# A PSUM bank for the weight conversion and a new interleaving of layers 3 and 4, in a fused attention and MLP kernel

## The chip, the cores and the metric

The kernel runs on one core of a Trainium2 chip, as one launch. The metric is the device time of the launch in microseconds (us). Three runs before gave 752.56 us as median (752.18 to 753.29).

The engines are named as in the profile: PE is TensorE (matmuls; PEld its weight loads), DVE is VectorE, ACT is ScalarE, POOL is GpSimd, SP is SyncE, which here only issues DMAs. SBUF is the large on-chip memory, PSUM the small one of eight banks of 128 x 512 fp32 into which PE writes. Each engine works through its own instructions strictly in the order of the program and waits where an input, or a buffer, isn't ready.

## What is computed

Batch 2, 8 heads, 768 positions, head size 64: an attention in which a query sees only the keys of its own hash bucket, and then two MLPs on 1536 tokens of width 512. The weights come as float64.

```python
attn = softmax(where(bucket(q) == bucket(k), q @ k.T / 8, -1e9)) @ v   # 16 heads
x = attn, heads side by side                                           # 1536 x 512
h = maximum(maximum(x @ w1, x @ w2), x @ w3)                           # 1536 x 768   "layer 1"
x = h @ w_out                                                          # 1536 x 512   "layer 2"
u = x @ w_in                                                           # 1536 x 2048  "layer 3"
g = where(u >= 1, u, where(u <= -1, 0, (u + 1) ** 2 / 4))
out = g @ w_out2                                                       # 1536 x 512   "layer 4"
```

## The kernel before

**Precision.** Every fp32 factor is split into a high part (a cast to the fast matmul type fp32r) and a low part (the rest), and each product is three matmuls: high x high, high x low, low x high (`PARTS`, `mm3`). A high part is made by ACT, the low part by POOL, which subtracts.

**Weights.** There are 58 slices of a weight matrix, 128 x 512 or 128 x 384, in the order in which they are needed: 18 of layer 1, 8 of layer 2, then by turns two of layer 3 and two of layer 4. `w_steps(n)` turns one from float64 into fp32 parts. It is a generator that stops (`yield`) after each instruction or two, and `w_tick(k)`, called at many places of the program, runs k of these pieces, so conversion is strewn into the other work. A slice takes: a DMA of the raw slice (L196, two raw buffers), ACT's square of the upper words into the tile `wg` (L208), four DVE instructions (L210, L215, L219, L223), ACT's cast to the high part (L231), POOL's subtraction to the low part (L262). `wg` has two buffers in SBUF, the result `wg2` too; finished slices lie in seven buffers (`w`, `wx`), and `w_done` says which are free again. `w_get` converts at once what isn't ready when a product wants it.

**Block products.** The last 14 slices of layer 1 and all of layer 3 are done in pairs of slices by a scheme with seven products instead of eight. `pair_units` has eleven units of six matmuls; I number them u0 to u10. They need sums and differences of the two weight slices (`sr`, DVE, L242 to L247; split by ACT L254 and POOL L256 into two tiles `s`) and of the tokens (`x_d`). Between the units partial results move: u0's bank is copied by ACT into a second one (L1046); u3's goes to `x7` (L1057); DVE adds `x7` to the bank of u4 and so makes the start of u9 (L1062), before u7 may write that bank again; after u7 ACT copies its bank, for u10 (L1072). A tile `s` is not written before `w_state["open"]` allows it, and until then no further slice is begun (L249).

**Layers 3 and 4.** Nine steps (L1248). Step i does pair i of layer 3 (`l3`) and, for pair i-1, the twelve token tiles of layer 4 (`l4`, six matmuls each; I call them T0 to T11), which are added up in SBUF in `acc`. A string of 3s and 4s (L1253) sets the order of units and tiles. g is made of each layer 3 result by ACT (L1191, L1192), DVE (L1193), ACT (L1202) and POOL (L1203). Of a step's twelve tiles DVE adds eight to `acc` (L1238). The other four (`SEEDED`) go another way: ACT copies the old sum into the bank (L1222), the matmuls add to it there, and ACT copies the bank back (L1236).

**Banks.** After the attention PE's outputs rotate through eight PSUM banks, `b0` to `b5`, `u_ps` and `pj_ps`; `bank()` takes the one that has been free longest.

**Start.** After the attention layer 1's first four slices are multiplied plainly (`l1`, L1117), three chunks of tokens each, while `steps` (L1098) makes the token differences: two of them per chunk.

## Time and profile before

| | |
|---|---|
| median of three runs | 752.56 us |
| the profiled execution, its own time | 752.83 us |
| its span, first to last instruction | 750.8 us |
| PE busy | 671.3 us (89%) |
| DVE, ACT, POOL busy | 536.2, 428.9, 367.9 us (71, 57, 49%) |
| mean granted TensorE clock | 0.952 of full |
| attention, to the first unit of layer 1 | about 0 to 205 us |
| layer 1, plain part and seven pairs | 205 to 380 us |
| layer 2 | 380 to 429 us |
| layers 3 and 4 | 429 to 751 us |

PE's share is high everywhere, so what counts is where it waits, and where it runs at a lower granted clock; both are read by stretches. The views that answer this are the table of stretches (busy time and granted clock), PE's waits with what ended them, and the timeline. What an instruction costs is read from the groups by line and shape.

### The profile page before, as it was taken

How to read it: one execution, taken by the hardware profiler on the slowest of the kernel's cores; microseconds unless marked ns; L12 is line 12 of the kernel's file. 1: busy time of each engine (PE TensorE's matmuls, PEld its weight loads, DVE VectorE, ACT ScalarE, POOL GpSimd, SP SyncE). 2: the span in 40 equal slices, each digit the busy share in tenths (PEclk: the TensorE clock that was granted, in tenths of full speed). 3: DMA queues.
4: the chain of work that ended last, by engine and by line, in shares of the span. 5: the costliest groups of instructions: out<-in, count | busy, mean ns of one | idle time of the engine just before them, and what ended most of it. 6: DMA issues, size and time to landing. Idle time of an engine off the chain costs nothing.

```text
span 750.8 us, 11606 instructions
## 1 busy us (share of the span) xinstructions
PE 671.3 (89%) x4323; PEld 524.3 (70%) x4323; DVE 536.2 (71%) x775; ACT 428.9 (57%) x796; POOL 367.9 (49%) x313
## 2 busy tenths in 40 slices
PE   7999999999999489889899983989798989898998
PEld 5667777778787367667688862867576767676776
DVE  5788899998549688897755874675767676666633
ACT  7787778877622435444433563665556565646562
POOL 6435575653324764664343465353635363626340
PEclk9999999999999799999999996989899999899999
DMA  7856776862321112112202011111120202021004
GB/s 194 207 145 183 199 203 191 240 158 82 86 71 57 56 57 84 57 56 64 82 24 85 28 57 56 57 56 57 33 81 28 85 28 85 28 67 46 29 0 169
DMA packets 27856, 66.99 MB, mean 89 GB/s; under 512 B 4164, under 2 KB 9124, under 8 KB 27800
## 3 DMA queue, kind: packets, MB, share of 16 engines
q1 hardware_dynamic: 27488, 66.21, 29.7%
q8 instruction: 34, 0.56, 0.3%
q14 instruction: 22, 0.18, 0.1%
q10 hardware_dynamic: 312, 0.04, 0.0%
HBM read 46.17 MB, written 3.19 MB: 66 GB/s over the span
## 4 chain that ended last, share of the span: by engine, by line
PE 50%; DVE 22%; ACT 16%; POOL 6%; issue 5%; DMA 0%; DVEq 0%; ACTq 0%; POOLq 0%
PE b L299 13%; PE s_ps L440 5%; PE b L1230 5%; PE t_ps L473 5%; DVE wg L223 5%; PE u_ps L534 5%; DVE wg L210 5%; PE s_ps L443 4%; DVE wg L219 4%; DVE wg L215 4%; ACT r L1191 3%; PE u_ps L1230 3%; ACT wg L208 2%; PE u_ps L501 2%; ACT r L1192 2%
## 5 line engine op out<-in xcount | busy, mean ns | idle before, releaser
L1203 POOL TENSOR_TENSOR g<-r,g 128x512 fp32r<-128x512 f32 x48 | 66.1, 1378 | 92.7 <-ACT g L1202 75.1
L210 DVE SCALAR_TENSOR_TENSOR wg<-wg,wr 128x512 f32<-128x512 f32 (+1 forms) x58 | 68.0, 1173 | 53.7 <-ACT wg L208 53.6
L450 DVE TENSOR_SCALAR_CACHE_REDUCE p<-s_ps 128x768 f32<-128x768 f32 x96 | 89.8, 951 | 13.3 <-PE s_ps L443 9.9
L465 ACT ACTIVATE p<-p,nm 128x768 f32<-128x768 f32 x96 | 89.7, 936 | 6.8 <-DVE p L450 6.3
L440 PE MATMUL s_ps<-lo,q 128*128 128x384 f32 x192 | 72.5, 378 | 2.9 <-POOL lo L407 2.0
L299 PE MATMUL b<-x_d,s 128*128 128x512 f32 x204 | 56.1, 415 | 21.3 <-DVE b L1062 7.5
L299 PE MATMUL b<-x_hl,wx 128*128 128x512 f32 x288 | 74.2, 402 | 0.6 <-POOL wx L262 0.6
L1230 PE MATMUL b<-w,g 128*128 128x512 f32 (+1 forms) x207 | 56.3, 407 | 17.6 <-ACT w L231 10.1
L299 PE MATMUL b<-x_hl,w 128*128 128x512 f32 (+1 forms) x324 | 71.3, 371 | 0.0
L299 PEld LDWEIGHTS b<-x_hl,wx 128*128 128x128 f32 x288 | 56.8, 198 | 13.6 <-POOL wx L262 1.0
L262 POOL TENSOR_TENSOR wx<-wg,wx 128x512 fp32r<-128x512 f32 (+1 forms) x32 | 44.8, 1399 | 43.6 <-ACT wx L231 41.6
L443 PE MATMUL s_ps<-hi,q 76*128 76x384 f32 x192 | 66.1, 344 | 0.0
L299 PEld LDWEIGHTS b<-x_hl,w 128*128 128x128 f32 x324 | 56.7, 191 | 10.9 <-issue 0.6
L299 PEld LDWEIGHTS b<-x_d,s 128*128 128x128 f32 x204 | 39.7, 199 | 33.3 <-DVE b L1062 9.2
L1230 PE MATMUL b<-wx,g 128*128 128x512 f32 x159 | 48.0, 436 | 15.7 <-ACT b L1222 13.2
L219 DVE SCALAR_TENSOR_TENSOR wg<-wg,wg 128x512 int32<-128x512 int32 (+1 forms) x58 | 59.3, 1023 | 1.2
L1230 PEld LDWEIGHTS b<-w,g 128*128 128x128 f32 x207 | 39.8, 196 | 27.8 <-ACT w L231 10.5
L1193 DVE SCALAR_TENSOR_TENSOR r<-r,b 128x512 f32<-128x512 f32 x36 | 24.6, 684 | 47.4 <-ACT r L1192 47.4
L231 ACT CAST wx<-wg 128x512 fp32r<-128x512 f32 (+1 forms) x32 | 19.3, 603 | 66.2 <-DVE wg L223 66.2
L256 POOL TENSOR_TENSOR s<-sr,s 128x512 fp32r<-128x512 f32 x30 | 42.6, 1432 | 24.8 <-ACT s L254 24.8
L223 DVE SCALAR_TENSOR_TENSOR wg<-wr,wg 128x512 int32<-128x512 int32 (+1 forms) x58 | 53.1, 916 | 1.2
L215 DVE TENSOR_SCALAR wg<-wg 128x512 int32<-128x512 int32 (+1 forms) x58 | 49.2, 847 | 3.5
(184 smaller groups left out, 1596.7 us busy)
## 6 DMA issues: line engine op xcount, KB each, us to landing
wr<-in_w SPq DMA_DIRECT2D x48, 512.0 KB
r<-in_kq SPq DMA_DIRECT2D x15, 384.0 KB
q<-hi SPq DMA_DIRECT2D x15, 384.0 KB
v<-in_v SPq DMA_DIRECT2D x21, 256.0 KB
rb<-d SPq DMA_DIRECT2D x16, 192.0 KB
wr<-in_w SPq DMA_DIRECT2D x8, 384.0 KB
q<-lo SPq DMA_DIRECT2D x15, 192.0 KB
lo<-hi SPq DMA_DIRECT2D x15, 192.0 KB
```

The source lines that it names most:

```text
L210: nc.vector.scalar_tensor_tensor(out=f32(g), in0=f32(g), scalar=TINY_SQ, in1=f32(high), op0=ALU.is_ge, op1=ALU.mult)
L215: nc.vector.tensor_scalar(out=g2, in0=g, scalar1=3, scalar2=0x3FFFFFF8, op0=ALU.logical_shift_left, op1=ALU.bitwise_and)
L219: nc.vector.scalar_tensor_tensor(out=g2, in0=g, scalar=-0x40000000, in1=g2, op0=ALU.bitwise_and, op1=ALU.bitwise_or)
L223: nc.vector.scalar_tensor_tensor(out=g2, in0=low, scalar=29, in1=g2, op0=ALU.logical_shift_right, op1=ALU.bitwise_or)
L262: nc.gpsimd.tensor_tensor(out=w[:, 1, 0:cols], in0=f32(g2), in1=f32(w[:, 0, 0:cols]), op=ALU.subtract)
L299: nc.tensor.matmul(out=outp, lhsT=w_[a], rhs=x_[b_], start=(begins and i == 0 and jj == 0), stop=(ends and i == n - 1 and jj == 2), skip_g ...
L440: nc.tensor.matmul(out=o, lhsT=hd["qa"][:, qs], rhs=hd["lo"][:, ks], start=True, stop=False)
L443: nc.tensor.matmul(out=o, lhsT=hd["qb"][0:76, qs], rhs=hd["hi"][0:76, ks], start=False, stop=True)
L450: nc.vector.tensor_scalar(out=p.rearrange("p (a k) -> p a k", a=2), in0=s_ps[bank.at][:, :, 0:HALF], scalar1=MASKED, scalar2=MASKED, op0=A ...
L465: nc.scalar.activation(out=p, in_=p, func=ACTF.Exp, scale=-1.0, bias=tl[n]["nm"], accum_out=sums_of(h // 2)[:, c:c + 1],)
L1203: nc.gpsimd.tensor_tensor(out=lo, in0=r, in1=f32(hi), op=ALU.subtract)
L1230: nc.tensor.matmul(out=pb[:, cs], lhsT=gs[f][:, a, tsl], rhs=wt[:, b_, cs], start=(n == 0 and k not in seeds), stop=(n == len(terms) - 1), ...
```

## The change

Four things are changed.

1. The bank `pj_ps` leaves the rotation, which then has seven banks, and takes the place of `wg`: the square and the first results of DVE lie in it. L219's result now goes there as well, and the last DVE instruction reads it from there. In the attention, where `pj_ps` is in use, `wg` stays in SBUF, with one buffer.
2. The split of a pair's sums is taken out of `w_steps` into a queue of its own (`sums_todo`), of which each `w_tick` runs a piece when `open` allows it. Slices go on being converted meanwhile, up to the next one that would fill `sr`.
3. There are no seeded tiles: layer 4's tiles are added by DVE, all twelve of a step (in the first, i = 0, ACT copies them, as before).
4. The string changes: units stand two by two between single tiles, and eight tiles come after the last unit, where it was one by one and four. Each unit of layer 3 is followed by two ticks, where it was two or one. In layer 1's start there are three token steps per chunk in place of two, and two ticks in place of three for the first four.

```diff
-        g = w_p.tile([128, 512], I32, tag="wg", name="wg", bufs=2)[:, 0:cols]
+        g = w_state["bank"]
+        if g is None:
+            g = w_p.tile([128, 512], I32, tag="wg", name="wg", bufs=1)
+        g = g[:, 0:cols]
...
-            out=g2, in0=g, scalar=-0x40000000, in1=g2, op0=ALU.bitwise_and, op1=ALU.bitwise_or
+            out=g, in0=g, scalar=-0x40000000, in1=g2, op0=ALU.bitwise_and, op1=ALU.bitwise_or
...
-            out=g2, in0=low, scalar=29, in1=g2, op0=ALU.logical_shift_right, op1=ALU.bitwise_or
+            out=g2, in0=low, scalar=29, in1=g, op0=ALU.logical_shift_right, op1=ALU.bitwise_or
...
-        yield
-        while pair_at[n] >= w_state["open"]:
-            yield
-        s_ = [w_state["sums"].tile([128, 2, 2, 256], F32R, tag="s", name="s") for _ in range(2)]
-        sums_w[pair_at[n]] = s_
+        sums_todo.append((pair_at[n], sums_parts(pair_at[n], sr)))
+
+    def sums_parts(m, sr):
+        s_ = sums_w[m] = [w_state["sums"].tile([128, 2, 2, 256], F32R, tag="s", name="s") for _ in range(2)]
         for i in range(2):
...
+    def sums_tick():
+        if sums_todo and sums_todo[0][0] < w_state["open"] and next(sums_todo[0][1], 0) == 0:
+            sums_todo.pop(0)
...
     def w_tick(count=1):
         for _ in range(count):
+            sums_tick()
...
+                if n in pair_at and sums_todo:
                     return
...
-            for n, tile_ in ((6, u_ps), (7, pj_ps)):
-                at_bank[n] = tile_
-                banks.append(n)
+            at_bank[6] = u_ps
+            banks.append(6)
+            w_state["bank"] = i32(pj_ps)
...
-                    l1(j, w, c, slice(S - TCH, TCH) if (j, w, c) in early else slice(0, TCH))
-                    for _ in range(2):
+                    l1(j, w, c, slice(S - TCH, TCH) if (j, w, c) in early else slice(0, TCH), 2 if n < 4 else 3)
+                    for _ in range(3):
...
-                SEEDED = (1, 4, 7, 10)
...
-                        if k + 1 in SEEDED and i > 0:
-                            seeds[k + 1] = bank(True)
-                            nc.scalar.copy(out=seeds[k + 1][1], in_=acc[:, TOKS[k + 1]])
...
-                            if i == 0 or k in seeds:
+                            if i == 0:
                                 nc.scalar.copy(out=acc[:, t, cs], in_=pb[:, cs])
...
-                    for n, x in enumerate("33433434343434343434444"):
+                    for n, x in enumerate("33343343343343343444444" + "4"):
                         next(g3 if x == "3" else g4, None)
                         if x == "3":
-                            w_tick(2 - n % 2)
+                            w_tick(2)
```

The order of instructions up to layer 1 stays as it was. Lines after the change are some ten further down: L208 to L223 are L211 to L226 there, L1062 is L1072, L1238 is L1242.

DVE, at layer 1's start, where the fourth slice is converted (its raw words are `wr_2630`) and the token differences `raw` begin; before:

```order
L210 SCALAR_TENSOR_TENSOR wg_2926<-wg_2926,wr_2630 128x512
L215 TENSOR_SCALAR wg2_2929<-wg_2926 128x512
L219 SCALAR_TENSOR_TENSOR wg2_2929<-wg_2926,wg2_2929 128x512
L223 SCALAR_TENSOR_TENSOR wg2_2929<-wr_2630,wg2_2929 128x512
L1094 TENSOR_TENSOR raw_2904<-x_hl_72 128x1024
L1094 TENSOR_TENSOR raw_2905<-x_hl_72 128x1024
L960 TENSOR_TENSOR h1_2811<-b1_2813,h1_2811 128x256
```

and after:

```order
L213 SCALAR_TENSOR_TENSOR pj_ps_84<-pj_ps_84,wr_2630 128x512
L1104 TENSOR_TENSOR raw_2904<-x_hl_72 128x1024
L218 TENSOR_SCALAR wg2_2945<-pj_ps_84 128x512
L222 SCALAR_TENSOR_TENSOR pj_ps_84<-pj_ps_84,wg2_2945 128x512
L1104 TENSOR_TENSOR raw_2905<-x_hl_72 128x1024
L1027 TENSOR_TENSOR raw_2906<-raw_2904,raw_2906 128x1024
L1027 TENSOR_TENSOR raw_2904<-raw_2905,raw_2904 128x1024
L969 TENSOR_TENSOR h1_2811<-b1_2813,h1_2811 128x256
L226 SCALAR_TENSOR_TENSOR wg2_2945<-wr_2630,pj_ps_84 128x512
```

The slice's last DVE instruction has moved behind five others, four of them token differences of 1024 columns.

PE, at the end of step 4 of layers 3 and 4, before from u8 on and after the change from u9 on (`x_hl` and `x_d` are tokens, `s` sums, `w` and `wx` slices); before:

```order
L299 MATMUL pj_ps<-x_hl,wx 128x512 x6
L1230 MATMUL b_2863<-w,g 128x512 x6
L299 MATMUL b_2813<-x_hl,wx 128x512 x6
L1230 MATMUL b_2849<-w,g 128x512 x6
L299 MATMUL b_2833<-x_hl,s 128x512 x6
L1230 MATMUL u_ps<-w,g 128x512 x6
L1230 MATMUL b_2908<-w,g 128x512 x6
L1230 MATMUL b_2798<-w,g 128x512 x6
L1230 MATMUL pj_ps<-w,g 128x512 x6
```

and after:

```order
L308 MATMUL b_2833<-x_hl,wx 128x512 x6
L308 MATMUL b_2813<-x_hl,s 128x512 x6
L1235 MATMUL b_2849<-w,g 128x512 x6
L1235 MATMUL b_2798<-w,g 128x512 x6
L1235 MATMUL b_2863<-w,g 128x512 x6
L1235 MATMUL u_ps<-w,g 128x512 x6
L1235 MATMUL b_2908<-w,g 128x512 x6
L1235 MATMUL b_2833<-w,g 128x512 x6
L1235 MATMUL b_2813<-w,g 128x512 x6
L1235 MATMUL b_2849<-w,g 128x512 x6
```

The last unit (the one with `x_hl,s`) has moved ahead of four more tiles, and the tiles use the bank `pj_ps` no more.

DVE, in the same part of a step (acc is layer 4's sum); before:

```order
L210 SCALAR_TENSOR_TENSOR wg_5480<-wg_5480,wr_5402 128x512
L1238 TENSOR_TENSOR acc_4322<-u_ps_83,acc_4322 128x512
L215 TENSOR_SCALAR wg2_5491<-wg_5480 128x512
L1238 TENSOR_TENSOR acc_4322<-b5_2908,acc_4322 128x512
L219 SCALAR_TENSOR_TENSOR wg2_5491<-wg_5480,wg2_5491 128x512
L223 SCALAR_TENSOR_TENSOR wg2_5491<-wr_5402,wg2_5491 128x512
L1238 TENSOR_TENSOR acc_4322<-pj_ps_84,acc_4322 128x512
```

and after:

```order
L213 SCALAR_TENSOR_TENSOR pj_ps_84<-pj_ps_84,wr_5290 128x512
L1242 TENSOR_TENSOR acc_4300<-b3_2849,acc_4300 128x512
L218 TENSOR_SCALAR wg2_5407<-pj_ps_84 128x512
L222 SCALAR_TENSOR_TENSOR pj_ps_84<-pj_ps_84,wg2_5407 128x512
L226 SCALAR_TENSOR_TENSOR wg2_5407<-wr_5290,pj_ps_84 128x512
L1242 TENSOR_TENSOR acc_4300<-b0_2798,acc_4300 128x512
L1242 TENSOR_TENSOR acc_4300<-b4_2863,acc_4300 128x512
L1242 TENSOR_TENSOR acc_4300<-u_ps_83,acc_4300 128x512
```

Three additions now follow each other where two stood apart, and each conversion instruction has one operand in `pj_ps`.

## Rows read from the trace of the kernel before

**Rows 1.** The page, part 4: the chain that ended last, by engine.

```profile
PE 50%; DVE 22%; ACT 16%; POOL 6%; issue 5%; DMA 0%; DVEq 0%; ACTq 0%; POOLq 0%
```

**Rows 2.** Stretches: start:end, length, busy us (instructions) by engine, PEclk, DMA, GB/s.

```profile
230.90:271.15 40.25, 26.87 (x99) 20.47 (x97) 30.29 (x40) 15.87 (x26) 22.44 (x14) 0.83 0.18 61
271.15:378.30 107.15, 95.45 (x397) 76.03 (x396) 89.28 (x109) 46.69 (x87) 60.30 (x44) 0.97 0.20 66
378.30:428.62 50.32, 50.32 (x223) 41.70 (x222) 33.33 (x41) 19.49 (x36) 21.76 (x16) 1.00 0.16 50
428.62:446.84 18.22, 15.84 (x67) 12.16 (x66) 14.03 (x18) 11.16 (x20) 10.46 (x8) 1.00 0.18 59
446.84:496.25 49.41, 36.23 (x140) 28.11 (x138) 28.16 (x34) 30.18 (x54) 26.53 (x21) 0.83 0.13 43
496.25:543.58 47.33, 37.66 (x140) 28.85 (x138) 30.90 (x40) 26.67 (x47) 20.98 (x16) 0.86 0.16 56
543.58:696.91 153.33, 135.27 (x554) 108.13 (x552) 103.69 (x140) 91.10 (x160) 71.76 (x52) 0.94 0.16 55
696.91:750.80 53.89, 48.56 (x217) 39.46 (x215) 22.53 (x33) 24.57 (x44) 14.54 (x11) 1.00 0.18 69
```

**Rows 3.** PE's waits from 543.58 to 696.91: us in total, times, longest.

```profile
PE b L1230 <- ACT b L1222: 13.9, 4, 3.5
PE u_ps L1230 <- ACT u_ps L1222: 4.1, 4, 1.0
```

**Rows 4.** The timeline, PE: start, length, what [idle before <- what ended it].

```profile
459.86 0.80 PE L1230 MATMUL b<-w,g 128*128 128x512 f32 x1 [10.11 <-ACT w L231]
...
577.21 4.61 PE L1230 MATMUL b<-wx,g 128*128 128x512 f32 x12 [3.49 <-ACT b L1222]
...
705.11 1.52 PE L299 MATMUL b<-x_d,s 128*128 128x512 f32 x6
706.47 1.52 PE L1230 MATMUL pj_ps<-wx,g 128*128 128x512 f32 x6
```

**Rows 5.** PE's waits in layer 1 from 230.9 to 378.3.

```profile
PE b L299 <- DVE b L1062: 7.5, 4, 2.5
PE b L299 <- POOL s L256: 5.9, 1, 5.9
PE b L299 <- ACT s L254: 4.4, 1, 4.4
PE b L299 <- ACT b L1072: 3.6, 3, 2.4
PE b L299 <- DVE pj_ps L1062: 2.0, 1, 2.0
```

**Rows 6.** DVE's groups from 205 us on, by shape: out<-in xcount | busy us, mean ns.

```profile
L210 DVE SCALAR_TENSOR_TENSOR wg<-wg,wr 128x512 f32<-128x512 f32 x47 | 55.5, 1182 | 41.8 <-ACT wg L208 41.6
L219 DVE SCALAR_TENSOR_TENSOR wg<-wg,wg 128x512 int32<-128x512 int32 x47 | 51.3, 1091 | 1.0
L223 DVE SCALAR_TENSOR_TENSOR wg<-wr,wg 128x512 int32<-128x512 int32 x47 | 46.3, 986 | 1.0
L215 DVE TENSOR_SCALAR wg<-wg 128x512 int32<-128x512 int32 x47 | 39.5, 841 | 2.6
L1193 DVE SCALAR_TENSOR_TENSOR r<-r,b 128x512 f32<-128x512 f32 x36 | 24.6, 684 | 47.4 <-ACT r L1192 47.4
L1238 DVE TENSOR_TENSOR acc<-b,acc 128x512 f32<-128x512 f32 x29 | 19.9, 685 | 18.3 <-PE b L1230 18.3
...
L1062 DVE TENSOR_TENSOR b<-b,x 128x512 f32<-128x512 f32 x11 | 7.6, 690 | 0.8 <-ACT x L1057 0.6 <-PE b L299 0.2
...
L1018 DVE TENSOR_TENSOR raw<-raw 128x1024 f32<-128x1024 f32 x4 | 4.9, 1220 | 0.0
```

**Rows 7.** The timeline of one step, DVE and POOL.

```profile
589.30 1.29 POOL L1203 TENSOR_TENSOR g<-r,g 128x512 fp32r<-128x512 f32 x1 [5.94 <-ACT g L1202]
589.35 1.78 DVE L223 SCALAR_TENSOR_TENSOR wg<-wr,wg 128x512 int32<-128x512 int32 x1
...
595.94 0.68 DVE L223 SCALAR_TENSOR_TENSOR wg<-wr,wg 128x512 int32<-128x512 int32 x1
...
598.56 0.41 DVE L244 TENSOR_TENSOR sr<-wg,sr 128x256 f32<-128x256 f32 x1
598.89 0.41 DVE L246 TENSOR_TENSOR sr<-wg 128x256 f32<-128x256 f32 x1
```

**Rows 8.** The timeline at layer 1's start.

```profile
222.36 5.39 POOL L1094 TENSOR_TENSOR raw<-x_hl 128x1024 f32<-128x1024 f32 x2
...
222.98 2.51 DVE L215 TENSOR_SCALAR wg<-wg 128x512 int32<-128x512 int32 x1
...
231.04 2.90 PE L299 MATMUL u_ps<-x_hl,wx 128*128 128x512 f32 x12
```

**Rows 9.** The page, part 5: ACT's cast and POOL's subtraction.

```profile
L262 POOL TENSOR_TENSOR wx<-wg,wx 128x512 fp32r<-128x512 f32 (+1 forms) x32 | 44.8, 1399 | 43.6 <-ACT wx L231 41.6
...
L231 ACT CAST wx<-wg 128x512 fp32r<-128x512 f32 (+1 forms) x32 | 19.3, 603 | 66.2 <-DVE wg L223 66.2
```

More of the change, by code (lines that the diff above doesn't have):

```diff
@@ L178, in lsh_attention_moe_kernel @@
     pair_at = {key_index[b_]: m for m, (_, b_) in enumerate(PAIRS)}
-    g2s, sums_w = {}, {}
-    w_state = {"open": 0, "raw": 0, "done": 0, "base": 0, "gen": None, "auto": False, "more": None}
+    g2s, sums_w, sums_todo = {}, {}, []
+    w_state = {"open": 0, "bank": None, "raw": 0, "done": 0, "base": 0, "gen": None, "auto": False, "more": None}
     def w_piece(n, i):
@@ L271, in w_tick @@
                 if n >= NSL or n >= w_state["base"] + (WBUFS if w_state["more"] else WEARLY):
+                    return
+                if n in pair_at and sums_todo:
                     return
@@ L964, in l1_out, with l1 @@
                     pending.append(lambda: split_h(j, c))
-            def l1(j, w, c, cs=slice(0, TCH)):
+            def l1(j, w, c, cs=slice(0, TCH), ticks=3):
                 wt = w_get(("1", j, w))
@@ L973, in l1 @@
                 free(b, cs.stop - cs.start == TCH)
-                w_tick(3)
+                w_tick(ticks)
             def split_h(j, c):
@@ L1030, in pair_units @@
                 wts = [w_get(k) for k in keys]
-                assert m in sums_w
+                while m not in sums_w or sums_todo and sums_todo[0][0] == m:
+                    sums_tick()
                 s_ = sums_w.pop(m)
@@ L1216, in l4 @@
                     wts = [w_get(("4", f)) for f in fs]
-                    seeds = {}
                     for k, t in enumerate(TOKS):
                         tsl = slice(t * 128, (t + 1) * 128)
-                        if k + 1 in SEEDED and i > 0:
-                            seeds[k + 1] = bank(True)
-                            nc.scalar.copy(out=seeds[k + 1][1], in_=acc[:, TOKS[k + 1]])
                         cuts_ = 2 if i == 7 and k == NT // 128 - 1 else 1
                         for h in range(cuts_):
-                            b = seeds[k] if k in seeds else bank()
+                            b = bank()
                             pb = b[1]
@@ L1231, in l4 @@
                                     out=pb[:, cs], lhsT=gs[f][:, a, tsl], rhs=wt[:, b_, cs],
-                                    start=(n == 0 and k not in seeds), stop=(n == len(terms) - 1),
-                                    skip_group_check=k in seeds,
+                                    start=(n == 0), stop=(n == len(terms) - 1),
                                 )
-                            if i == 0 or k in seeds:
+                            if i == 0:
                                 nc.scalar.copy(out=acc[:, t, cs], in_=pb[:, cs])
```

## The prediction

> **What bounds the kernel now.** The chain that ended last gives PE half of the span, and DVE with ACT 38% [rows 1]: stretches in which PE works alternate with stretches in which it waits for the other two. So I priced PE's work and looked in which stretch more time than that goes by. A unit or a tile is six matmuls; one begins at 705.11 and the next at 706.47, in a stretch with the granted clock at 1.00, so six cost 1.36 us [rows 4]. [...]
>
> Against that stand, by the table of stretches [rows 2]: steps 3 to 6, 153.3 us for 4 x 31.28 = 125.1, so 28.2 over (A). Step 2, 47.3 for 31.3, 16.0 over (B). Step 1, 49.4, 18.1 over (C). Step 0, 18.2 for 11 units or 15.0, 3.3 over (D). Six pairs of layer 1, 107.1 for 66 units or 89.8, 17.4 over (E). The end of layer 1's plain part with its first pair (three chunks of twelve matmuls and ten units, 8.2 + 13.6 = 21.8), 40.2, 18.5 over (F). Layer 2 loses nothing: 50.3 us, all of it busy. The end from 696.9 on waits 2 to 3 us (G), as an estimate from the seed waits of the steps ahead of it.
>
> What is waited for: in A, PE is idle for 153.3 - 135.3 = 18.0 us, and two rows hold it all, 13.9 + 4.1 us in eight waits for L1222, ACT's copies of seeds [rows 3]. The other 10.1 us of A are matmuls at a lower granted clock, 0.94 in the mean. [...] A microsecond waited thus costs another 10.1 / 18.0 = 0.56. In C one wait of 10.11 us is for the first slice of layer 4 [rows 4]. In E and F PE waits for the sums (5.9 and 4.4 us) and for the partial results that DVE and ACT move (7.5, 2.0 and 3.6) [rows 5].
>
> **The change, edit by edit.** *No seeds.* The 28 tiles lose two ACT copies each, and DVE gets 28 additions. The waits of rows 3 go whole, with the clock that they cost. What is late next? The loads of a step answer. ACT has 91.1 / 4 = 22.8 us, less 8 copies at its mean of 91.1 / 160 = 0.57, so 18.2; POOL 71.8 / 4 = 17.9 [rows 2]. DVE will have 16 conversion instructions at 0.69 (next paragraph), 12 additions at 0.685, 6 L1193 at 0.684, one L1062 at 0.69 and four sums at 0.41 [rows 6, 7]: 11.0 + 8.2 + 4.1 + 0.7 + 1.6 = 25.7. All lie under 31.3, so PE becomes the bound, if what it waits for is queued early enough.
>
> *Conversion in a bank.* A slice's four DVE instructions now take 1.18 + 0.84 + 1.09 + 0.99 = 4.10 us in the mean [rows 6]. They are long because two operands in SBUF make DVE wait while POOL runs: L223 took 1.78 us beside POOL's L1203 and 0.68 when POOL was idle [rows 7]. Instructions with one operand in PSUM stand at 0.684 to 0.690 throughout (L1193, L1238, L1062), POOL or not [rows 6]. With the bank each of the four has an operand there. Two of them, L213 and L222, read and write one bank in place, which no row shows. The bounds are L1062, which reads one bank and writes another, 0.69, and the 1.22 us of a 1024-column instruction, as if the two passes followed each other [rows 6]. I take 0.69, since L1062 is the nearest. A slice then takes 2.76, 1.34 less. One buffer in place of two for `wg` loses nothing: one slice is converted at a time, and its square came after the last slice's L223 already.
>
> [...]
>
> *The string.* Units no longer stand one by one with tiles, so each result of layer 3 is split by DVE, ACT and POOL earlier, and eight tiles with 8 x 0.685 us of additions cover 8 x 1.36 us of PE behind them. In a walk along DVE's queue as it is written, DVE comes back to the same place of the next step after 30.8 us if independent instructions start 0.08 us before their forerunner ends (598.89 against 598.56 + 0.41 [rows 7]), and after 33.8 if each waits for the last one's end. So A's loss is 0 to 2.5 us a step; I take 1.0, nearer to the overlap that the row shows, and 4 for A (from 28.2). B has the same, and a tail of C's delay: 1.5 (0 to 4).
>
> For C: the first tile is now behind three units, not two, so it is wanted 1.36 us later, and two slices come 1.34 earlier each. The wait falls from 10.1 to about 6.0, with clock lost 7 in all. If all four slices' gain counts it is 10.1 - 1.4 - 5.4 = 3; with none, 8.7 and a little over 2 of clock, 11. D: 1 (0 to 3).
>
> *Sums queued.* Slices go on while `s` is taken, and the sums' parts no longer stand in a slice's way. In E DVE has 89.3 of 107.1 us [rows 2]; 15 slices at 1.34 less leave 69 of 90. Its queue then has slack, and L1062 waits less. L1072 and other copies of ACT remain. I take 0.8 us a pair, 5 in all. Bounds: 0, and 12, the pairs' waits for DVE and ACT as they are (17.4 less the 5 that slack in a queue gives back at least).
>
> *Start.* Three token steps per chunk push DVE's L226 of the fourth slice behind three differences. L215 began at 222.98 while POOL was on 222.36 to 227.75, and took 2.51 us [rows 8]. In that place now come L1104 1.22, L218 0.69, L222 0.69, L1104 1.22, two L1027 2.44, a 256-column addition, at half of 0.69 about 0.34, and L226 0.69: 7.3 us, so 230.3, and up to 4.8 more if the first one has to wait for POOL. Cast and subtraction add 0.60 + 1.40 [rows 9]: 232.3 to 237.0, and PE wants the slice at 231.04 [rows 8]. That is a new stall of 1 to 6 us; I take 4. The waits for sums, 5.9 + 4.4 [rows 5], mostly go, since they are made while chunks run: 1 left. With 5 for matmuls at the lower clock behind both (the granted clock there is 0.83 [rows 2]) F is 10 (5 to 16). G: 0.5 (0 to 2).
>
> **Sum.** From 28.2 to 4, 16.0 to 1.5, 18.1 to 7, 3.3 to 1, 17.4 to 5, 18.5 to 10, 2.3 to 0.5: 103.8 becomes 29, a gain of 75. The profiled execution's own time of 752.8 (its span is 750.8) agrees with the median of 752.6, so both give 678. All lows together (8) give 657, all highs (10 + 4 + 11 + 3 + 12 + 16 + 2 = 58) 707.
>
> **Rivals.** *Seven banks.* `pj_ps` leaves the rotation, so a bank is wanted again 7 x 1.36 = 9.5 us after it was taken, not 10.9. Eight tiles in a row all need DVE, whose queue has a slice (2.76) or a pair's sums between the additions; where it lags, the next step's u0 waits for the bank of a tile. For it: a step has 25.7 us of DVE in a strict order, and the slower walk was late there. Against: after a slice's four instructions come three additions in a row, 2.1 us for 4.1 of PE. If it holds, the slower walk's 2.5 us a step come over what I took, in six steps 16: 694. [...]
>
> *DVE as slow as before.* The conversion may still wait for POOL, or the in-place ones cost 1.22. Then a slice stays near 4.1, DVE's step is 25.7 + 4 x 1.34 = 31.1, with 41.8 / 47 = 0.9 us of idleness ahead of each L210 [rows 6] 34.7. That is 3.4 over PE's, 5.3 with the clock at 0.56, so 4.3 more than taken in six steps and 6 in the pairs: 710. Against it stand the even 0.68 to 0.69 of all rows with a bank.
>
> *It doesn't do what it says.* Seed waits may only be the visible end of another lag, and steps stay at 38.3: A keeps 28.2 and B much of its loss, so 678 + 24 + 14 = 716. Against: rows 3 hold A's whole idle time, and what is left for ACT and DVE is under PE's work.
>
> *Slower.* It decides in L213 and L222, eight a step: from 0.69 + (38.3 - 25.7) / 8 = 2.3 us each DVE alone fills the 38.3 us that a step takes now, and layer 1's 30 of them make 69 + 30 x 1.6 = 117 us for 107. From there on the kernel is slower than before; at 2.4 us, 39.4 a step and 120 in layer 1 give about 770. Against: no DVE row of 512 columns with a bank in [rows 6] is over 0.69.
>
> **How the numbers follow.** Forecast, 678: 0.70, its own range 657 to 707. Seven banks, 694: 0.12. DVE as slow as before, 710: 0.10. Not what it says, 716: 0.04. Slower, 770: 0.04. The range 657 to 712 holds most of the first and the next two. About 0.2% is what a measurement of this kernel can tell; faster than that holds for all but the slower case and its border: 0.95, within it 0.01, slower 0.04.
>
> **What would show it.** In the changed kernel's profile: L213, L218, L222 and L226 at 0.68 to 0.71 us in the mean; a step's first matmuls 31.3 to 34 us apart; no wait on an ACT copy in the steps, and a granted clock of 0.97 or more; T0 of step 1 waiting 4 to 6 us for a slice; a wait of 1 to 6 us near 231 at the fourth slice's first chunk; pairs 15 to 16 us apart. I am wrong if PE waits for DVE's additions or a bank in each step (seven banks), if the four stay at 0.8 to 1.2 (DVE as slow), or if the in-place ones stand above 1.2.

## The result, and the profile after

The changed kernel takes 672.85 us (median of four runs, 671.09 to 674.23) against 752.92 us: a ratio of 0.8933, with an interval of 0.8905 to 0.8961. The profiled execution has 671.09 us of its own, and a span of 669.3 us where it was 750.8. The prediction was 678, between 657 and 712.

The chain that ended last is now mostly PE's own work, where [rows 1] gave it half:

```profile
PE 79%; DVE 12%; ACT 4%; issue 3%; DMA 1%; POOL 1%; DVEq 0%; ACTq 0%; SPq 0%; POOLq 0%
```

The table of stretches, cut at the same places of the program as [rows 2] (columns as there):

```profile
230.03:260.66 30.63, 25.98 (x97) 19.64 (x96) 27.78 (x37) 15.48 (x26) 20.08 (x12) 0.89 0.26 86
260.66:355.28 94.62, 90.49 (x397) 74.28 (x397) 70.21 (x111) 48.15 (x90) 57.52 (x45) 1.00 0.23 74
355.28:405.60 50.32, 50.32 (x224) 41.67 (x222) 30.32 (x43) 19.53 (x37) 20.13 (x16) 1.00 0.18 57
405.60:423.52 17.92, 15.83 (x67) 12.23 (x66) 13.20 (x20) 12.01 (x23) 12.62 (x10) 1.00 0.12 42
423.52:461.91 38.39, 33.85 (x139) 27.17 (x138) 22.73 (x36) 30.46 (x57) 25.74 (x21) 0.91 0.24 76
461.91:493.19 31.28, 31.28 (x139) 25.90 (x138) 22.89 (x37) 20.45 (x37) 16.82 (x13) 1.00 0.23 76
493.19:618.31 125.12, 125.12 (x553) 103.60 (x552) 97.71 (x157) 73.33 (x128) 67.31 (x52) 1.00 0.21 68
618.31:669.30 50.99, 47.83 (x217) 39.67 (x215) 27.46 (x43) 15.21 (x26) 12.98 (x10) 1.00 0.17 63
```

Steps 2 to 6 take 31.28 us each, and PE is busy for all of it at a granted clock of 1.00: exactly 23 times 1.36 (11 units and 12 tiles). Against [rows 2] the stretches give back, in order, 9.6, 12.5, 0, 0.3, 11.0, 16.0, 28.2 and 2.9 us; with 0.9 ahead of the first that is the 81.5 by which the span is shorter. ([rows 2] begins its first stretch 0.3 us before the end of the chunk at which this table begins; cut alike, that stretch gives 9.3.) The loads of a step came out near those forecast: in steps 3 to 6 ACT is busy for 18.3 us a step (forecast 18.2), POOL for 16.8 (17.9) and DVE for 24.4 (25.7).

What PE still waits for from 200 us on (total, times, longest):

```profile
PE b L1235 <- ACT wx L234: 3.3, 1, 3.3
PE b L308 <- DVE u_ps L1072: 2.6, 2, 2.2
PE b L308 <- DVE b L1072: 1.9, 1, 1.9
PE u_ps L308 <- ACT wx L234: 1.9, 1, 1.9
PE b L1235 <- POOL wx L268: 1.3, 1, 1.3
PE b L308 <- ACT x_hl L1163: 1.2, 1, 1.2
...
PE u_ps L308 <- POOL wx L268: 0.9, 1, 0.9
```

No wait is for a layer 4 addition, or for a bank of the rotation that isn't free yet. Those for L1072, and the two left out for L1056 and L1082 (1.2 and 0.2 us), are for links between the units of a pair. DVE's groups from 200 us on answer [rows 6]: the four conversion instructions, 0.68 to 0.70 us each where they stood at 0.84 to 1.18:

```profile
L222 DVE SCALAR_TENSOR_TENSOR pj_ps<-pj_ps,wg 128x512 int32<-128x512 int32 x47 | 32.8, 697 | 1.2
L213 DVE SCALAR_TENSOR_TENSOR pj_ps<-pj_ps,wr 128x512 f32<-128x512 f32 x47 | 32.7, 697 | 30.0 <-ACT pj_ps L211 30.0
L218 DVE TENSOR_SCALAR wg<-pj_ps 128x512 int32<-128x512 int32 x47 | 32.3, 687 | 2.3
L226 DVE SCALAR_TENSOR_TENSOR wg<-wr,pj_ps 128x512 int32<-128x512 int32 x47 | 32.2, 684 | 1.1
```

### The profile page after: what moved, and what is told of

It reads as the page before. It is cut to its first block, busy times and chain, and to the rows that moved or that the text cites. A ratio compares the mean times of both kernels' runs of the same rounds, so it can differ in the third digit from the quotient of the medians.

```text
span 669.3 us, 11587 instructions
## 1 busy us (share of the span) xinstructions
PE 645.2 (96%) x4323; PEld 513.4 (77%) x4323; DVE 495.6 (74%) x803; ACT 396.6 (59%) x740; POOL 352.8 (53%) x313
## 4 chain that ended last, share of the span: by engine, by line
PE 79%; DVE 12%; ACT 4%; issue 3%; DMA 1%; POOL 1%; DVEq 0%; ACTq 0%; SPq 0%; POOLq 0%
PE b L308 24%; PE b L1235 18%; PE u_ps L308 7%; PE s_ps L449 6%; PE t_ps L482 5%; PE u_ps L543 5%; PE s_ps L452 5%; PE u_ps L510 3%; DVE raw L1027 2%; PE u_ps L1235 2%; PE pj_ps L425 2%; DVE pj_ps L213 1%; DVE wg L226 1%; DVE wg L218 1%; DVE pj_ps L222 1%
## 5 line engine op out<-in xcount | busy, mean ns | idle before, releaser
L459 DVE TENSOR_SCALAR_CACHE_REDUCE p<-s_ps 128x768 f32<-128x768 f32 x96 | 89.7, 951 | 13.3 <-PE s_ps L452 10.0
L1213 POOL TENSOR_TENSOR g<-r,g 128x512 fp32r<-128x512 f32 x48 | 62.7, 1306 | 37.9 <-ACT g L1212 37.7
L308 PE MATMUL b<-x_d,s 128*128 128x512 f32 x270 | 68.6, 398 | 6.4 <-DVE u_ps L1072 2.6
L1235 PE MATMUL b<-wx,g 128*128 128x512 f32 x264 | 67.5, 393 | 4.5 <-ACT wx L234 3.3
L308 PEld LDWEIGHTS b<-x_d,s 128*128 128x128 f32 x270 | 51.2, 192 | 19.6 <-DVE u_ps L1072 3.4
L213 DVE SCALAR_TENSOR_TENSOR pj_ps<-pj_ps,wr 128x512 f32<-128x512 f32 (+1 forms) x55 | 37.2, 677 | 37.5 <-ACT pj_ps L211 37.5
L234 ACT CAST wx<-wg 128x512 fp32r<-128x512 f32 (+1 forms) x32 | 19.4, 605 | 73.3 <-DVE wg L226 73.3
L1235 PEld LDWEIGHTS b<-wx,g 128*128 128x128 f32 x264 | 49.8, 189 | 15.7 <-ACT wx L234 3.7
L268 POOL TENSOR_TENSOR wx<-wg,wx 128x512 fp32r<-128x512 f32 (+1 forms) x32 | 40.7, 1273 | 39.3 <-ACT wx L234 36.1
L308 PE MATMUL b<-x_hl,w 128*128 128x512 f32 (+1 forms) x282 | 59.5, 363 | 0.0
L1242 DVE TENSOR_TENSOR acc<-b,acc 128x512 f32<-128x512 f32 (+1 forms) x77 | 51.6, 677 | 8.9 <-PE b L1235 8.9
L449 PEld LDWEIGHTS s_ps<-lo,q 128*128 128x128 f32 x192 | 36.7, 191 | 21.3 <-DVE p L459 8.6
L492 ACT COPY pt<-t_ps 128x768 f32<-128x768 f32 (+1 forms) x59 | 41.0, 706 | 17.0 <-PE t_ps L482 14.7
L268 POOL TENSOR_TENSOR w<-wg,w 128x512 fp32r<-128x512 f32 (+1 forms) x26 | 33.0, 1269 | 29.9 <-ACT w L234 26.8
```

The source lines that it names most:

```text
L213: nc.vector.scalar_tensor_tensor(out=f32(g), in0=f32(g), scalar=TINY_SQ, in1=f32(high), op0=ALU.is_ge, op1=ALU.mult)
L268: nc.gpsimd.tensor_tensor(out=w[:, 1, 0:cols], in0=f32(g2), in1=f32(w[:, 0, 0:cols]), op=ALU.subtract)
L308: nc.tensor.matmul(out=outp, lhsT=w_[a], rhs=x_[b_], start=(begins and i == 0 and jj == 0), stop=(ends and i == n - 1 and jj == 2), skip_g ...
L449: nc.tensor.matmul(out=o, lhsT=hd["qa"][:, qs], rhs=hd["lo"][:, ks], start=True, stop=False)
L459: nc.vector.tensor_scalar(out=p.rearrange("p (a k) -> p a k", a=2), in0=s_ps[bank.at][:, :, 0:HALF], scalar1=MASKED, scalar2=MASKED, op0=A ...
L492: copy(out=grp[g][:, 3 * a:3 * b_, r * 128:(r + 1) * 128].rearrange("p (a j) q -> p a j q", a=b_ - a), in_=t_ps[:, a:b_, 0:HALF].rearrange ...
```

## The experiments

Every kernel was cut at the same matmuls, so a difference can be put down to a stretch. This table holds the length of each in the profiled execution (worked out from the starts of the matmuls in the timelines; F from the end of the chunk before it, the letters as in the prediction), and the median of the timed runs. F begins 230.0 to 233.8 us into the span, from profile to profile, which says nothing here. Where kernels run the same instructions in a stretch, its length agrees within 0.1 us (F and E of the changed kernel, a_seeds and i_step0).

| kernel | F | E | D | C | B | A | G | median us |
|---|---|---|---|---|---|---|---|---|
| before | 39.9 | 107.2 | 18.2 | 49.4 | 47.3 | 153.3 | 53.8 | 752.9 |
| changed | 30.6 | 94.6 | 17.9 | 38.4 | 31.3 | 125.1 | 50.9 | 672.9 |
| b_bank | 32.2 | 89.8 | 15.7 | 46.8 | 39.7 | 137.6 | 53.0 | 698.4 |
| b_noseeds | 39.9 | 105.8 | 18.2 | 49.4 | 38.0 | 146.6 | 57.3 | 742.6 |
| a_nobank | 40.2 | 107.9 | 20.2 | 44.5 | 35.9 | 134.7 | 51.4 | 717.7 |
| a_seeds | 30.6 | 94.6 | 17.9 | 38.5 | 38.7 | 153.8 | 52.6 | 711.4 |
| a_order | 31.1 | 95.7 | 19.0 | 41.3 | 32.3 | 130.2 | 52.2 | 684.8 |
| a_sums | 31.9 | 92.0 | 15.9 | 46.4 | 33.5 | 125.3 | 51.0 | 678.7 |
| a_start | 32.9 | 95.4 | 17.9 | 38.3 | 31.3 | 125.1 | 50.9 | 675.8 |
| a_sums_start | 32.1 | 89.8 | 15.9 | 45.5 | 33.5 | 125.3 | 51.3 | 678.8 |
| i_piece1 | 30.3 | 92.7 | 17.9 | 39.0 | 32.0 | 125.1 | 50.9 | 672.1 |
| i_t1 | 30.1 | 92.7 | 19.4 | 38.4 | 31.3 | 125.1 | 50.9 | 670.9 |
| i_step0 | 30.6 | 94.6 | 26.4 | 39.7 | 31.3 | 125.1 | 51.0 | 683.3 |
| i_best | 30.0 | 92.7 | 19.5 | 40.4 | 31.3 | 125.1 | 50.9 | 673.0 |

The kernels named b_ are the kernel before with one edit, those named a_ the changed kernel with an edit taken back, and those named i_ attempts at what is left.

### One edit alone

**b_noseeds.**

```diff
-                SEEDED = (1, 4, 7, 10)
...
-                            if i == 0 or k in seeds:
+                            if i == 0:
```

> The kernel before with one edit: no seeded tiles, DVE adds all twelve tiles of a step; conversion stays in SBUF, the string and the sums stay. Theory of the prediction (two causes add up: seed copies and slow conversion): the seed waits go, but DVE then has 25.7 + 4 x 1.34 = 31.1 us of work a step and 0.9 idle ahead of each slice, 34.7 in all, so steps come down from 38.3 to about 35 to 36 us and the kernel to 733 (725 to 742), with PE waiting for DVE's additions or for slices. Rival 'conversion alone': the seeds were late only because conversion is slow, so their removal gives nothing that DVE's extra additions don't take back, 745 to 757. Rival 'seeds alone': the steps reach 31.3 to 32.5, 710 or less.

It took 742.57 us (ratio 0.9849, 0.9816 to 0.9883), a little beyond the theory's range (742) and short of the rival "conversion alone" (745). Steps 3 to 6 gained 6.7 us and step 2 9.3, while the end (G) lost 3.4. Four of the six rows of PE's waits in its steps 3 to 6:

```profile
PE b L1224 <- ACT w L231: 4.4, 2, 2.5
PE pj_ps L1224 <- ACT wx L231: 2.6, 1, 2.6
PE pj_ps L1224 <- POOL wx L262: 2.0, 2, 1.1
PE b L1224 <- ACT wx L231: 1.8, 1, 1.8
```

The seed waits are gone, and tiles wait for their weights instead: 13.1 us with the two rows left out (1.4 and 0.9), every one ended by a cast or a subtraction of a slice. DVE converts late, as the theory had it, but what suffers is the slice and not the addition.

**b_bank.** The kernel before with the bank: conversion through `pj_ps`, as in the diff, and seven banks in the rotation.

> The kernel before with one edit: conversion through the PSUM bank (seven banks in the rotation); seeds, string and sums stay. Theory of the prediction: the seed waits of 18 us in steps 3 to 6 stay about as they are, since they are ACT's copies of old sums; the gain is in the pairs (12), at step 1 (4 to 8) and somewhat in layer 1's start, 728 (720 to 738). Rival 'conversion alone': ACT's queue holds the seeds back only behind casts that wait for DVE, so the steps fall to 32 to 33 us with the seeds in place, 690 or less. Rival 'seven banks': seeds hold two banks longer, and one bank less makes steps longer than 38.3, 745 or more.

It took 698.35 us (0.9272, 0.9241 to 0.9303), a far larger gain than the theory of two independent causes gave (720 to 738), and 8 us short of the rival's 690. Its pairs stand at PE's floor (the table of stretches, PE busy for all 89.79 us):

```profile
263.50:353.29 89.79, 89.79 (x397) 74.30 (x396) 66.97 (x110) 46.79 (x88) 55.32 (x44) 1.00 0.24 78
```

And in steps 3 to 6 the seed waits are still there, but halved, with none over 2.1 us:

```profile
PE b L1233 <- ACT b L1225: 7.5, 7, 2.1
PE u_ps L1233 <- ACT u_ps L1225: 2.1, 1, 2.1
```

So conversion is the larger cause, also of half of the seed waits in [rows 3] (18.0 us there, 9.6 here). Step 1 gained only 2.6 us: its first tile still waits 8.0 us for a slice.

### One edit taken back

**a_nobank.**

```diff
-        g = w_state["bank"]
-        if g is None:
-            g = w_p.tile([128, 512], I32, tag="wg", name="wg", bufs=1)
+        g = w_p.tile([128, 512], I32, tag="wg", name="wg", bufs=2)
```

(with L222 and L226 on `g2` again, and `pj_ps` back in the rotation)

> The changed kernel with one edit taken back: conversion in SBUF again (two buffers), eight banks in the rotation. Theory of the prediction: DVE's instructions wait for POOL again, a slice costs 4.1 us in the mean, DVE's step is 34.7 us and layer 1's pairs lose their gain: 700 to 712. Rival 'conversion alone': 730 or more. Rival that the string and the missing seeds give enough slack: within 5 us of the changed kernel, 673 to 678.

717.73 us (0.9529, 0.9500 to 0.9557), 6 us over the forecast. The bank is worth 45 us in the company of the other edits: 9.6 in F, 13.3 in E, 2.3 in D, 6.1 in C, 4.6 in B, 9.6 in A. F I had undervalued. DVE's slice took 1.07 + 0.67 + 0.81 + 0.81 = 3.36 us in steps 3 to 6, and PE waits there for DVE's L1062 and ACT's L1072 (L1069 and L1079 in this kernel), the links of the seven products, not for additions:

```profile
PE b L305 <- DVE b L1069: 2.8, 3, 0.9
PE b L305 <- ACT b L1079: 1.6, 3, 0.6
```

**a_seeds.**

```diff
+                        if k + 1 in SEEDED and i > 0:
+                            seeds[k + 1] = bank(True)
+                            nc.scalar.copy(out=seeds[k + 1][1], in_=acc[:, TOKS[k + 1]])
```

(and the rest of the seeded tiles as before)

> The changed kernel with one edit taken back: tiles 1, 4, 7 and 10 of a step are seeded by ACT again. Theory of the prediction: the seed waits come back where the tiles stand close together, most of 18 us and the clock behind them in steps 3 to 6, some in step 2: 695 to 710. Rival 'conversion alone': ACT isn't late any more once DVE is quick, so seeds cost nothing, 671 to 676.

711.39 us (0.9446, 0.9420 to 0.9472), 38.5 over the changed kernel, with steps 3 to 6 as long as in the kernel before (153.8 and 153.3), though conversion is quick. "ACT isn't late any more" is out. One of the waits, in the timeline of step 3:

```profile
527.54 0.62 ACT L211 ACTIVATE pj_ps<-wr 128x512 f32<-128x512 f32 x1
...
530.38 0.69 DVE L226 SCALAR_TENSOR_TENSOR wg<-wr,pj_ps 128x512 int32<-128x512 int32 x1
...
531.10 0.62 ACT L234 CAST w<-wg 128x512 fp32r<-128x512 f32 x1 [2.43 <-DVE wg L226]
531.63 0.58 ACT L1233 COPY u_ps<-acc 128x512 f32<-128x512 f32 x1
532.26 2.93 PE L1241 MATMUL u_ps<-wx,g 128*128 128x512 f32 x6 [4.71 <-ACT u_ps L1233]
```

The seed copy L1233 needs nothing but an old sum and a free bank. It stands in ACT's queue behind a cast, L234, that waits 2.43 us for a whole slice on DVE, and that slice's square, L211, came only after ACT's work on the last units. PE pays 4.71 us. The seed is late by what stands ahead of it on ACT, and the order of units sets that as much as the conversion does. The table tells which matters. With the old string seeds and conversion add up in A: 6.7 us (b_noseeds) and 15.7 (b_bank) make 22.4, and a_order below, which has both edits, gains 23.1. What doesn't add is seeds and string. Beside the bank, seeds cost 7.4 us in A with the old string (137.6 in b_bank, 130.2 in a_order) and 28.7 with the new one (153.8 and 125.1). a_order and a_seeds also have the queue of sums and the new start, which b_bank lacks; no run has seeds, the bank and the new string without them.

**a_order.**

```diff
-                    for n, x in enumerate("33343343343343343444444" + "4"):
+                    for n, x in enumerate("33433434343434343434444"):
...
-                            w_tick(2)
+                            w_tick(2 - n % 2)
```

> The changed kernel with one edit taken back: the string of units and tiles and the ticks of layers 3 and 4 are those of before. Theory of the prediction, as the first four runs have left it (seeds and slow conversion each cost something in the steps, and neither explains the 28 us alone): with both gone PE is close to the bound in any order, steps 3 to 6 take 125 to 131 us and the kernel 673 to 681. Rival 'order': the steps reach PE's floor only since eight tiles follow the last unit; with single tiles between single units they stay at 33 to 35 us, 683 to 700.

684.76 us (0.9100, 0.9071 to 0.9128). Steps 3 to 6 take 130.2 us, 32.6 each, inside the theory's range, while the whole is past it and in the rival's: the old string costs 5.1 in A, 2.9 in C, 1.3 in G and about 1 in B, D and E each. PE's waits in A are 3.4 us, all for POOL's half of a slice (L268). The string is worth some 12 us, and without it the steps still come within 1.3 us each of the floor.

**a_sums, a_start, a_sums_start.**

> The changed kernel with one edit taken back: the sums are split inside the conversion of a slice again, which waits there until a tile is free. Theory of the prediction: the queue lets sums of layer 1's first pairs come in time; without it PE waits 5 to 8 us for them at 245, 676 to 682, the steps of layers 3 and 4 as in the changed kernel. Rival: the queue itself shifts DVE's order in layer 1 (pairs 94.6 us, where the bank alone gives 89.8), so without it the pairs go to 90 and the time is 667 to 671.

> The changed kernel with one edit taken back: two token steps per chunk and three ticks, as before, at layer 1's start. Theory of the prediction: the wait for the fourth slice (1.9 + 0.9 us at 232) goes, and the sums come up to 8 us late at 245 instead: layer 1's plain end and first pair 30 to 33 us, 671 to 677. Rival: the three token steps shift all that follows, and without them the pairs go from 94.6 to 90: 666 to 670.

> The changed kernel with two edits taken back, the queue of sums and the start; what stays is the bank, the missing seeds and the new string. From the bank-only kernel's stretches (plain end and first pair 32.2 us, pairs 89.8, step 0 15.7) and the changed kernel's later steps (38.4, 31.3, 125.1, 50.9): 1.6 - 4.8 - 2.3 = 5.5 us less than the changed kernel, 667 (664 to 670). If one of the two edits is needed by the steps of layers 3 and 4 (sums there come late without the queue): 673 or more.

They took 678.68 (0.9024, 0.8991 to 0.9057), 675.75 (0.8985, 0.8960 to 0.9010) and 678.79 us (0.9021, 0.8997 to 0.9045). a_sums has the median that I expected and for another reason. Without the queue F loses 1.3 us, not 5 to 8, and E and D even gain 2.6 and 2.0, as the rival said (it put E at 90, and it came to 92.0); the cost is in C and B, 8.0 and 2.2 us, where the first slice of layer 4 comes late. Its square on ACT starts at 421.21, 0.2 us after step 1 began and behind the sums' casts (L257, from 418.25); in the changed kernel it starts at 417.39, 6.1 us before step 1. PE then waits:

```profile
PE b L1228 <- ACT w L234: 5.8, 1, 5.8
PE b L1228 <- ACT wx L234: 1.5, 1, 1.5
```

In a_start the fourth slice comes in time, and the sums are late instead, by 2.1 and 6.7 us near 245:

```profile
PE b L308 <- POOL s L258: 6.7, 1, 6.7
PE b L308 <- ACT s L256: 2.1, 1, 2.1
```

That is the theory's price (30 to 33 us for F, 671 to 677), and the pairs did not fall. In a_sums_start F, E and D came out as I had put them together from b_bank (32.1, 89.8, 15.9), and C and B lost about what a_sums lost there (7.1 and 2.2), so the case held in which the later steps need the queue. The queue of sums has a price in layer 1 of 2.6 us in E with the new start and 5.6 with the old one (94.6 against 92.0, 95.4 against 89.8) and 2 in D, and is paid back about twice in C and B.

### What is left

**i_piece1.** A part of the sums takes the place of a piece of conversion in a tick, up to step 1.

```diff
-            sums_tick()
+            if sums_tick() and "l3" not in w_state:
+                continue
```

(`sums_tick` tells whether it did a part; "l3" is set at step 1)

> The changed kernel, where until step 1 of layers 3 and 4 a piece of the queued sums takes the place of a piece of conversion in a tick instead of coming on top of it. Theory: what the queue cost in the pairs (94.6 us, 92.0 without it) and in step 0 (17.9, 15.9 without it) is that two pieces a tick put DVE's addition for the seventh product behind conversion instructions that wait for ACT; with one piece a tick the pairs take 90 to 92.5 us and step 0 15.7 to 16.5, the later steps stay: 668 (666 to 671). Rival: the loss is from slices converted ahead of the sums, whatever the ticks hold; pairs and step 0 as in the changed kernel, 672 to 674.

672.11 us (0.8937, 0.8891 to 0.8983). The pairs fell to 92.7, just past the theory's range, step 0 stayed at 17.9, and C and B took 1.3 back. The time can't be told apart from the changed kernel's. That the pairs fell because of one piece a tick isn't shown: i_t1, next, keeps two pieces a tick and has the same 92.7, from another order at the start alone. What step 0 loses by the queue stays open.

**i_t1.**

```diff
-..., 2 if n < 4 else 3)
+..., 3 if n == 1 else 2 if n < 4 else 3)
```

> The changed kernel with a third tick after the second chunk of layer 1's start, which puts the fourth slice's last DVE instruction ahead of the three differences instead of behind them. Theory of the prediction (the new stall is that instruction's place in DVE's queue): the waits of 1.9 and 0.9 us near 232 go, the differences and sums come 0.7 us later, layer 1's plain end and first pair take 27 to 29.5 us instead of 30.6: 670 (668 to 672). Rival: the wait only moves on to the sums, 30 us or more there and 672 to 675.

670.88 us (0.8915, 0.8883 to 0.8947), not to be told apart from the changed kernel. The time lies in the theory's range, but not for its reason. The wait at 232 went and came back 9 us later, at the next slice (the rival had put it at the sums), so F fell by 0.5 us only, to 30.1:

```profile
PE b L308 <- POOL wx L268: 2.4, 1, 2.4
PE b L308 <- ACT wx L234: 2.1, 1, 2.1
```

The rest is E, 1.9 us shorter, and D, 1.5 longer, neither of which either theory had.

**i_step0.**

```diff
-                            w_tick(2)
+                            w_tick(3 if i == 0 else 2)
```

> The changed kernel with three ticks instead of two after each unit of step 0 of layers 3 and 4, so that layer 4's first two slices are converted some units earlier. Theory: step 1's stall (3.3 + 1.3 us and the clock behind it, 38.4 us for 31.3) is the conversion's place behind ACT's work for the last units of step 0; step 1 falls to 32 to 35 us, step 0 grows by at most 1: 668.5 (666 to 671). Rival: ACT is the limit there (30.5 us of 38.4), the earlier casts push its other work back and step 1 stays within 1.5 us of 38.4: 671 to 674.

683.34 us (0.9086, 0.9049 to 0.9124), worse than either theory. Step 1's waits for weights did go, but step 1 is no shorter (39.7), and step 0 grew by 8.5 us. The timeline of step 0, ACT and PE's longest wait there, shows why:

```profile
415.70 0.62 ACT L234 CAST w<-wg 128x512 fp32r<-128x512 f32 x1 [2.95 <-DVE wg L226]
...
422.52 2.92 PE L308 MATMUL b<-x_d,s 128*128 128x512 f32 x6 [3.95 <-DVE b L1072]
...
423.82 0.62 ACT L234 CAST w<-wg 128x512 fp32r<-128x512 f32 x1 [2.95 <-DVE wg L226]
...
429.69 0.62 ACT L234 CAST wx<-wg 128x512 fp32r<-128x512 f32 x1 [2.95 <-DVE wg L226]
430.21 0.58 ACT L1082 COPY b<-b 128x512 f32<-128x512 f32 x1
```

With more ticks between units a slice's square and its cast stand next to each other in ACT's queue, and ACT stands still for the 2.95 us that the four DVE instructions between them take, with the units' work behind it (L1082 here). PE's wait of 3.95 us is for DVE's L1072 at 421.77. That stands in DVE's queue behind an L1203, which waited 1.94 us for ACT, and behind the next slice's L213, which waited for ACT's square.

**i_best.** i_t1, and in step 1 seven units ahead of the first tile.

```diff
-                    for n, x in enumerate("33343343343343343444444" + "4"):
+                    for n, x in enumerate("3333333433433434" + "4" * 8 if i == 1 else "33343343343343343444444" + "4"):
```

> The third tick of i_t1, and in step 1 of layers 3 and 4 seven units ahead of the first tile (then 4, 33, 4, 33, 4, 3 and nine tiles), all other steps as in the changed kernel. Theory: the tile waits in i_t1 until 432.5 for the second slice of layer 4, and four more units of 1.36 us stand ahead of it without moving any conversion behind ACT's work; step 1 falls from 38.4 to 32 to 34 us, and the kernel from i_t1's 670.9 to 666 (664 to 668). Rival, from the run with three ticks in step 0, where the wait for weights went and waits for ACT's copies and DVE's additions came in its place: step 1 stays at 37 us or more, 669 to 673.

672.99 us (0.8933, 0.8902 to 0.8963). Tiles don't wait any more in step 1, but units do, and it takes 40.4 us:

```profile
PE b L308 <- ACT b L1056: 2.6, 1, 2.6
PE b L308 <- DVE b L1072: 1.8, 1, 1.8
PE u_ps L308 <- ACT u_ps L1082: 0.6, 1, 0.6
```

The rival has it again. In step 1, where ACT is busy for 30.5 of 38.4 us, the stall moved with whatever was put first, in i_step0 and here. No kernel that was run beats the changed one measurably.

## Why the prediction was right

**The floor and the stretches.** Six matmuls at 1.36 us and the difference to it by stretch carried the sum. The losses that I left over, against those measured: A 4 and 0, B 1.5 and 0, C 7 and 7.1 (38.39 less 31.28), D 1 and 3.0, E 5 and 4.9, F 10 and 8.9. G gave 2.9 where I put 1.8. Steps 2 to 6 reach the floor, where I was too careful by 5.5 us; that is as much as the 5 us between 678 and the result, and the other differences about cancel.

**Three sizes are right in part by luck.** In E I expected ACT's copies to hold up each pair. What is left there is 2.2 + 1.9 us for DVE's addition L1072 and 0.2 for ACT, and it comes with the queue of sums, which I had put down as a gain: with the bank alone E stands at its floor of 89.8. In C the wait fell to 4.5 us where I had 6.0, and the lower clock (granted 0.91) cost 2.6 where I had 1. I took C's gain from the string and the slices' quicker conversion; the largest part taken back by one edit is the queue's (8.0 us, against 6.1 for the bank and 2.9 for the string). In F I gave the gain to the new start. Without the bank F gains nothing from it (40.2 in a_nobank, 39.9 before), and with the bank alone F is 32.2 already, where the new start and the rest make 30.6 of it.

**Conversion in a bank: right.** 0.684 to 0.697 for the four, 0.69 taken. The in-place ones stand 0.010 to 0.013 above the others, nowhere near the 1.22 of the other bound or the 2.3 from which the slower case began. One of the readings behind it was loose: POOL was idle only when the L223 of [rows 7] at 595.94 began. POOL's next instruction started while L223 ran, and took 1.59 us in place of 1.29 (the L219 at 594.73 took its 0.69 us with POOL idle throughout):

```profile
596.16 1.59 POOL L1203 TENSOR_TENSOR g<-r,g 128x512 fp32r<-128x512 f32 x1 [2.95 <-issue]
```

**No seeds: right in sum, wrong as a cause of its own.** The prediction gave A's 28 us to the seed waits and took the rest of the change as what keeps the place clear. The runs say for A: seeds gone alone 6.7 us, the bank alone 15.7, both with the old string 23.1 (a_order), all 28.2; and seeds put back into the changed kernel cost 28.7. In the whole kernel the bank alone is worth 54.6 of the 80.1 us, and the missing seeds alone 10.4. The step that failed is "the waits of rows 3 go whole, with the clock that they cost": with the seeds gone alone, 13.1 us of waits for slices take their place. The rival "DVE as slow as before" was this same dependence. Its price of 710 was 8 us short of a_nobank, and near it by luck: it put 26 us on six steps and 6 on the pairs, where a_nobank loses 20.3 in steps 1 to 6, 13.3 in the pairs and 9.6 in F, and no wait of PE there is for one of DVE's additions of layer 4.

**Clock.** I charged 0.56 us for each us waited. b_bank waited 9.6 us in A in pieces of at most 2.1, at a granted clock of 1.00, and PE's busy time was 3.0 over the floor; a_seeds waited 18.8 in pieces of up to 4.7, at 0.93, and was 9.8 over. So the charge is not the same for every wait. In the changed kernel C has 2.6 us for 4.5 waited (granted clock 0.91), which is the 0.56, and F 4.2 for 4.7 (0.89).

**The start: the stall is right as a place and a size.** The timeline of the changed kernel (PE, DVE, POOL):

```profile
221.18 6.73 POOL L1104 TENSOR_TENSOR raw<-x_hl 128x1024 f32<-128x1024 f32 x2
...
225.58 4.68 DVE L1027 TENSOR_TENSOR raw<-raw 128x1024 f32<-128x1024 f32 x2
...
230.51 0.68 DVE L226 SCALAR_TENSOR_TENSOR wg<-wr,pj_ps 128x512 int32<-128x512 int32 x1
...
231.89 0.73 PE L308 MATMUL u_ps<-x_hl,wx 128*128 128x512 f32 x2 [1.86 <-ACT wx L234]
...
233.51 4.63 PE L308 MATMUL u_ps<-x_hl,wx 128*128 128x512 f32 x10 [0.89 <-POOL wx L268]
```

The slice's last instruction starts at 230.51 behind two differences that take 4.68 us in place of 2.44 (POOL runs until 227.9), and PE waits 1.9 + 0.9 us, inside the 1 to 6 forecast. PE has no wait for sums left in F, where I had left 1 us. **Step 1** waited 3.3 + 1.3 us for its second slice, inside the 4 to 6.

**D was mis-sized.** I took 1 us and it lost 3.0. Its waits are 1.2 us for L1163, 0.6 for sums and 0.2 for L1164. b_bank, without the queue of sums, has only 0.4 for sums and takes 15.7, and a_sums the same 0.4 and 15.9. How the queue makes L1163 late stays open.

**The rival "seven banks"** has no wait of its kind in the changed kernel or in b_bank: steps 2 to 6 of the changed kernel have no wait at all. Small waits for a bank that ACT or DVE has yet to read out stand in steps 1 and 2 of a_sums and a_sums_start (0.9 to 1.0 us each) and of i_piece1 (0.3), but a_nobank, with eight banks, has some of 2.6 and 0.9 too. (Six times the 2.5 us of its sum is 15, not 16, so its time should have been 693.)

## What to carry to other kernels

Price the bound engine's work by stretch, and take what is over it, not busy shares: here the gain summed from seven such differences, 75, came within 7 us of the 81.5 in the span. Where a queue serves several chains, a late instruction is late by what is queued ahead of it, so what one edit is worth depends on the others. Here seeds cost 7.4 or 28.7 us in four steps, by the string, and the five edits taken back one at a time cost 104 us where all together they gave 80. Test each alone and each taken back. And an instruction that waits for another engine needs other work of its own engine between it and its forerunner: in i_step0, with little of it, casts behind four DVE instructions kept ACT still for 2.95 us each. More pieces at a time can be worse than fewer: with three ticks step 0 took 26.4 us, with two 17.9.

## What the runs showed of the hardware

**What still has two SBUF operands takes longer beside POOL, and the order sets how much.** The sums and token differences on DVE, which still read SBUF twice, became slower than before. In the changed kernel:

```profile
L247 DVE TENSOR_TENSOR sr<-wg,sr 128x256 f32<-128x256 f32 x15 | 16.1, 1073 | 0.5
...
L250 DVE TENSOR_TENSOR sr<-wg,sr 128x256 f32<-128x256 f32 x15 | 9.5, 633 | 0.0
...
L1027 DVE TENSOR_TENSOR raw<-raw 128x1024 f32<-128x1024 f32 x4 | 9.0, 2255 | 0.0
```

L1018 of [rows 6], the same instruction as this L1027, had 1.22, and I had taken 0.41 for each of the sums. It isn't the bank that lengthened them. The four sums of a pair take 2.02 us before, 2.05 with the bank alone and 2.78 in the changed kernel, but 2.75 in a_nobank too, which has the queue of sums and no bank. L1027 takes 2.26 with the bank and the new start, 1.77 with the new start alone (a_nobank), and 1.22 with the old start, bank or not (before, b_bank). POOL gains a little: its L1203 went from a mean of 1.378 to 1.306 us (L1213).

How much longer shows at single instructions of the changed kernel. The pair of L1027 that began at 225.58 took 4.68 us, 2.24 more than twice 1.22, and POOL's L1104 still ran for 2.33 us when it began. L247 took 0.42 to 0.43 us the three times that POOL did nothing beside it, and 1.24 in the mean of the twelve times that POOL ran.

**With its operand in PSUM the single-operand instruction has lost its speed.** L215 on SBUF alone takes 0.41 to 0.43 us where POOL is idle (21 of 48 in the kernel before, DVE's timeline from 200 us on; the other 27, beside POOL, take 1.16 in the mean, though they read only one operand), and L218, the same from the bank, 0.687:

```profile
233.36 0.43 DVE L215 TENSOR_SCALAR wg<-wg 128x512 int32<-128x512 int32 x1
```

So the bank makes one of the four instructions slower than it could be, by 0.26 us, and all four independent of POOL: in the changed kernel each of them takes 0.68 to 0.70 us (128 x 512), with POOL running beside it or not, and their means in b_bank are 0.68 to 0.70 too. Here the second was worth far more: the four take 2.77 us a slice where they took 4.10.
